# Attention units issued between the front products of the loop, and low halves of the first block kept off GpSimd

## Chip, core and metric

One Trainium2 chip, one NeuronCore. The metric is device time in microseconds (us), lower is better. The kernel is float32 throughout, with matrix products made from a high and a low float32r half of each operand.

## What is computed

Linear attention feeds two feed-forward layers. Per batch b and head h (8 x 8, sequence 576, head width 64):

```python
q_s = softmax(q, axis=-1)                  # over the 64 features
k_s = softmax(k, axis=2)                   # over the 576 positions
kv = einsum('bhsd,bhse->bhde', k_s, v)
x = einsum('bhsd,bhde->bhse', q_s, kv)     # heads side by side: 4608 x 512
x = (sigmoid(x @ w_gate) * (x @ w_val)) @ w_out        # 512 -> 1536 -> 512
h = x @ w_in                                           # 512 -> 2048
P = a0 + a1*h + a2*h**2 + a3*h**3;  Q = 1 + |b0|*|h| + |b1|*h**2
out = (P / (Q + 1e-6)) @ w_out2                        # 2048 -> 512
```

The weights arrive as float64; the kernel takes their bits apart on the chip.

## The kernel before

The 4608 tokens are cut into 9 blocks (j) of 512. A block of the first layer has 12 steps (f = 0 to 11, NF1 = 12). A step makes two front products, pg and pv, each summed over four chunks kk of the model width: 24 matmuls (`front_a`, 6 per chunk). ScalarE takes the sigmoid of pg, VectorE multiplies it with pv (the gate, L415), ScalarE rounds the result to its high half gh, and VectorE or GpSimd subtracts to get the low half gl (`vec_a`). The back product of the step before (12 matmuls, `back_a`) follows. pg and pv have two PSUM buffers in all, so the next step's front product can write pg only when the sigmoid has read it, and pv only when the gate has.

**The first block** and two blocks of attention are not written as a loop. Each piece of work is an op with predecessors, and a list scheduler at build time (`in_time`) puts them in order by a table of costs (`KINDS`). An op whose cost is a dict may go to VectorE or GpSimd: it takes the engine on which it would end first. That holds for k_sub, q_sub, q_div (softmax subtractions and divisions) and for the low halves w_l, g_l and next_l. In this block 36 weight pieces are unpacked: an absolute value on ScalarE, four bit operations on VectorE (L205, L208, L215, L218), a high half wh on ScalarE and a low half wl. The chosen engine shows at L472, which is the line of the helper that issues the op.

**The loop** runs steps i = 12 to 107. In step i the attention of a later block is worked on, four units u (pairs of heads) per block; `UNIT_STEPS` = 4, 6, 8, 10 sets the step d at which unit u is finished. All attention products share the two PSUM buffers of `ps_x`, in the order of issue. A unit has these parts: `load_k`, `load_q`, `load_v` (transfers on SP's queue), `att_km` (maximum of k, L287), `att_kt` (transpose ps_kt, then maximum mx L296 and a copy L298), `att_kb` (transpose back, then copy kma L306), `att_ks` (subtraction on GpSimd), `att_ke` (exponential of k, L327), `att_qm`, `att_qs`, `att_qe` (exponential of q, L319), `att_n` (four VectorE operations, L332 to L338), `att_kv` (20 matmuls, L353, L355, kvh on ScalarE, kvl on VectorE), `att_q` (four transposes ps_qt, high half qh, low half ql) and `att_d` (ps_xt and a copy into x_raw). The step issues them in this order:

```python
for kk in range(KC):
    front_a(f, kk, *ps)
vec = vec_a(j, f, *ps)
next(vec)                 # sigmoid
next(vec)                 # gate
run(sequence((), early_work.get(i, [])))                              # att_kt
run(prep(prep_at.get(i, [])), sequence(vec, work.get(i, [])))         # gh, gl, attention
if pend:
    back_a(*pend.pop(0))
run(sequence((), late_work.get(i, [])))                               # att_kb, att_ks
```

Beside it `prep` unpacks the 32 weight pieces of the second layer, spread over the loop; their low half hl is on GpSimd, and each is stored to memory by SP. The second layer follows the loop and is not touched.

Of the kernel before, what the change touches and what calls it, by code (L numbers as in the profile page):

```python
# [20 lines left out]
B, H, S, D = 8, 8, 576, 64  # L21
# [5 lines left out]
NF1, NF2 = F1 // P, F2 // P  # L27
# [11 lines left out]
PE, ACT, DVE, POOL, DMA = "PE", "ACT", "DVE", "POOL", "DMA"  # L39
# [8 lines left out]
    "x": (PE, 0.75), "x_h": (ACT, 0.6), "x_l": (DVE, 0.7),  # L48
    "xa": (PE, 0.65), "xa_out": (ACT, 0.25), "xb": (PE, 0.65), "xb_out": (ACT, 0.55),
    "w_abs": (ACT, 0.67), "w_clip": (DVE, 0.42), "w_cut": (DVE, 0.42), "w_low": (DVE, 0.7), "w_sign": (DVE, 0.7),  # L50
    "w_h": (ACT, 0.62), "w_l": ({DVE: 0.7, POOL: 1.29},),
    "front": (PE, 1.37), "sig": (ACT, 0.6, "sigmoid"), "gate": (DVE, 0.7), "g_h": (ACT, 0.63),
    "g_l": ({DVE: 0.7, POOL: 1.29},),
    "back": (PE, 2.73), "next_h": (ACT, 0.62), "next_l": ({DVE: 0.7, POOL: 1.29},),
}
LATENCY = {PE: 0.25, ACT: 0.2, DVE: 0.15, POOL: 0.15, DMA: 2.0}
TABLE_LOAD, TABLE_WEIGHT = 1.28, 2.0
# [61 lines left out]
def kernel(ctx: ExitStack, tc: tile.TileContext, q, k, v, w1, w2, ab_in, out):  # L119


    nc = tc.nc
# [9 lines left out]
    ps_x = ctx.enter_context(tc.tile_pool(name="ps_x", bufs=2, space=PSUM))  # L132
    dram = ctx.enter_context(tc.tile_pool(name="dram", bufs=1, space=DRAM))

    def f32(ap):
        return ap.bitcast(F32)
# [19 lines left out]
    w2_d = [dram.tile([P, 2, NB], F32, name=f"w2_{p}") for p in range(2 * NF2)]  # L156
    x3_d = [dram.tile([KC, P, NB], F32, name=f"x3_{j}") for j in range(NBLK)]

    def split_steps(h, lo, src, lo_eng):
        nc.scalar.activation(h, src, AF.Copy)  # L160
        yield
        lo_eng.tensor_tensor(out=lo, in0=src, in1=f32(h), op=ALU.subtract)  # L162
# [5 lines left out]
    def mm3(ps, wh, wl, xh, xl, first, last):  # L168
        nc.tensor.matmul(ps, wh, xh, start=first, stop=False)  # L169
        nc.tensor.matmul(ps, wl, xh, start=False, stop=False)  # L170
        nc.tensor.matmul(ps, wh, xl, start=False, stop=last)  # L171
# [13 lines left out]
    NW1, NW = 3 * NF1, 3 * NF1 + 2 * NF2  # L185
    raw, val, wt = {}, {}, {}
# [35 lines left out]
    def prep_split(p, eng=nc.gpsimd):  # L222
        if p < NW1:
            wt[p] = [wpool.tile([P, NB], F32R, tag="w", name=n) for n in ("wh", "wl")]
            yield from split_steps(*wt[p], val.pop(p), eng)
        else:
            hl = stage.tile([P, 2, NB], F32R, tag="raw", name="hl")
            yield from split_steps(hl[:, 0], hl[:, 1], val.pop(p), nc.gpsimd)
            yield
            nc.sync.dma_start(out=w2_d[p - NW1], in_=f32(hl))  # L230

    def fetch(p):
        wt[p] = [wpool.tile([P, NB], F32R, tag="w", name=n) for n in ("wh", "wl")]
        for n in range(2):
            nc.sync.dma_start(out=f32(wt[p][n]), in_=w2_d[p - NW1][:, n])

    def prep(stage_of):

        for p, n in stage_of:
            yield from (prep_load, prep_abs, prep_bits_a, prep_bits_b, prep_split)[n](p) or ()  # L240
            yield

    def mix(*jobs):
# [7 lines left out]
    def run(*jobs):  # L251

        jobs = list(jobs)
        while jobs:
            for x in list(jobs):
                if next(x, jobs) is jobs:
                    jobs.remove(x)

    def wa(f, i):
        return wt[at1[f, i]]  # L260
# [144 lines left out]
    def front_a(f, kk, pg, pv):  # L405
        for i, ps in enumerate((pg, pv)):
            wh, wl = wa(f, i)
            s = slice(kk * P, (kk + 1) * P)
            mm3(ps, wh[:, s], wl[:, s], x_h[:, kk, :], x_l[:, kk, :], kk == 0, kk == KC - 1)

    def vec_a(j, f, pg, pv):
        sg = tmp.tile([P, NB], F32, tag="t0", name="sg", bufs=1)
        nc.scalar.activation(sg, pg, AF.Sigmoid)  # L413
        yield
        nc.vector.tensor_tensor(out=sg, in0=pv, in1=sg, op=ALU.mult)  # L415
        yield
        gh = tmp.tile([P, NB], F32R, tag="gh", name="gh")
        gl = tmp.tile([P, NB], F32R, tag="gl", name="gl")
        g_t["a", j, f] = (gh, gl)
        late = nc.gpsimd if j == NBLK - 1 and f < NF1 - 1 else nc.vector  # L420
        yield from split_steps(gh, gl, sg, late if j else Chosen(("g_l", f)))

    def back_a(j, f):
        if f == 0:
            accs["a", j] = [ps_acc.tile([P, NB], F32, tag="acc", name="acc") for _ in range(KC)]
        gh, gl = g_t.pop(("a", j, f))
        wh, wl = wa(f, 2)
        for m, n in order(f == NF1 - 1):
            x, y = ((wh, gh), (wl, gh), (wh, gl))[n]
            nc.tensor.matmul(  # L430
                accs["a", j][m], x[:, m * P:(m + 1) * P], y, start=(f == 0 and n == 0),
                stop=(f == NF1 - 1 and n == 2))
        if f == NF1 - 1:
            for m, acc in enumerate(accs.pop(("a", j))):
                if m % 2:
                    nc.vector.tensor_copy(out=x_raw[:, m, :], in_=acc)  # L436
                else:
                    nc.scalar.activation(x_raw[:, m, :], acc, AF.Copy)
                nc.sync.dma_start(out=x3_d[j][m], in_=x_raw[:, m, :])
# [35 lines left out]
    for i in range(2 * NHP):  # L475
        j, u = divmod(i, NHP)
# [81 lines left out]
    for o in in_time(ops, chosen):  # L558
        ops[o][0]()

    work, early_work, late_work = {}, {}, {}

    def at(step, fn, *args):
        work.setdefault(max(step, NF1), []).append((fn, args))

    for j in range(2, NBLK):
        for u in range(NHP):
            d = NF1 * (j - 1) + UNIT_STEPS[u]
            if (j, u) != (2, 0):
                at(d - 5, load_k, j, u) if j < B else None  # L570
                at(d - 5, load_q, j, u)
            if j < B:
                at(d - 4, att_km, j, u)
                early_work.setdefault(max(d - 3, NF1 + 1), []).append((att_kt, (j, u, ps_x, "x")))
                late_work.setdefault(max(d - 3, NF1 + 1), []).append((att_kb, (j, u, ps_x, "x")))
                late_work[max(d - 3, NF1 + 1)].append((att_ks, (j, u, nc.gpsimd)))
                at(d - 2, att_ke, j, u)
                at(d - 3, load_v, j, u)
                at(d - 1, att_kv, j, u)
            at(d - 4, att_qm, j, u)  # L580
            at(d - 4, att_qs, j, u, nc.vector)
            at(d - 2, att_qe, j, u)
            at(d - 2, att_n, j, u, nc.vector)
            at(d - 1, att_q, j, u)
            at(d, att_d, j, u)

    def split_x():
        for kk in range(KC):
            split(x_h[:, kk, :], x_l[:, kk, :], x_raw[:, kk, :], nc.vector)

    def sequence(first, calls):
        yield from first
        for fn, args in calls:
            yield from fn(*args) or ()
            yield


    prep_at = {}
    for p in range(NW1, NW):
        at0 = NF1 + 2 + 5 * (p - NW1) // 2  # L600
        for n, step in enumerate((0, 1, 1, 2, 2)):
            prep_at.setdefault(at0 + step, []).append((p, n))

    NA = NBLK * NF1
# [1 line left out]
    for i in range(NF1, NA):  # L606
        j, f = divmod(i, NF1)
        ps = ps_f.tile([P, NB], F32, tag="f", name="pg"), ps_f.tile([P, NB], F32, tag="f", name="pv")
        for kk in range(KC):
            front_a(f, kk, *ps)  # L610
        vec = vec_a(j, f, *ps)
        next(vec)
        next(vec)
        if i == NF1:
            nc.scalar.activation(babs, ab[:, 4:6], AF.Abs)
        if i == NA - 1:
            nc.scalar.preload_act_table_set("natural_log_exp_and_others")
        if f == NF1 - 1:
            split_x()
        run(sequence((), early_work.get(i, [])))  # L620
        run(prep(prep_at.get(i, [])), sequence(vec, work.get(i, [])))
        if pend:
            back_a(*pend.pop(0))
        run(sequence((), late_work.get(i, [])))
        pend.append((j, f))
        if j == NBLK - 1 and f == 4:
            nc.sync.dma_start(out=x_raw, in_=x3_d[0].rearrange("m p c -> p m c"))
        if i == NA - NF1 - 2:
            att_ctx.close()
        if j == NBLK - 1:  # L630
            while len(wt) < NW and order1[len(wt) - NW1][0] < f - 1:
                fetch(len(wt))
# [84 lines left out]
    for i in range(NBS + LAG):  # L717
        while len(wt) < NW and i >= 0 and order1[len(wt) - NW1][0] < NF1 + i - 1:
            fetch(len(wt))
        if i < NBS:  # L720
            j, f = divmod(i, NF2)
# [57 lines left out]
```

## Time and profile before

| | us |
|---|---|
| median of 3 runs (range) | 1834.70 (1833.99 to 1836.22) |
| profiled execution, its own time | 1834.72 |
| its span, first to last instruction | 1832.9 |
| TensorE matmuls busy in the span | 1772.1 (97%) |
| VectorE busy | 1182.3 (65%) |
| ScalarE busy | 1005.6 (55%) |
| GpSimd busy | 363.3 (20%) |

PE is TensorE's matmuls, PEld its weight loads, DVE VectorE, ACT ScalarE, POOL GpSimd, SP the queue that issues transfers. A share of the whole span averages three stages that have different limits: the first block, the loop, and the second layer. Times of the trace count from the first instruction.

### The profile page before, as it was taken

To read this page: it belongs to the slowest core of one execution; us is meant where nothing else is said; L and a number is where in the kernel's file an instruction comes from. 1 tells how busy PE (TensorE), PEld (TensorE's weight loads), DVE (VectorE), ACT (ScalarE), POOL (GpSimd) and SP (SyncE) were. 2 spreads that over 40 slices of the span, in tenths; PEclk is the share of its full clock that TensorE was granted. 3 is DMA by queue.
4 is the path that set the end of the run, shared out by engine and by line. 5 is a ranking of instruction groups with operands and counts; after the bars stand their busy time and mean duration, and the time that the engine had idled before them with its cause. 6 is when DMAs were issued, how large, how long until landed. Compare 5 with 4: busy or idle time off the path is not lost.

```text
span 1832.9 us, 22295 instructions
## 1 busy us (share of the span) xinstructions
PE 1772.1 (97%) x8384; PEld 1452.7 (79%) x8384; DVE 1182.3 (65%) x1925; ACT 1005.6 (55%) x1652; POOL 363.3 (20%) x279
## 2 busy tenths in 40 slices
PE   5988999999999999999999999999999999999999
PEld 3766787787888878778888888888888888888887
DVE  9998545445455454454430288888888888887876
ACT  4556443444435354443331387777676777777765
POOL 3543010101011010110001122222222222222222
PEclk7999999999999999999999999999999999999999
DMA  6442323223132321312226401010000000000000
GB/s 206 146 150 89 115 68 107 69 64 114 62 123 75 110 79 54 123 61 84 78 77 212 160 24 43 5 47 12 35 23 24 24 24 24 23 24 24 1 24 23
DMA packets 53388, 129.54 MB, mean 71 GB/s; under 512 B 5664, under 2 KB 5664, under 8 KB 53280
## 3 DMA queue, kind: packets, MB, share of 16 engines
q1 hardware_dynamic: 53280, 128.12, 21.0%
q8 instruction: 66, 1.08, 0.2%
q14 instruction: 42, 0.34, 0.1%
HBM read 92.44 MB, written 35.65 MB: 70 GB/s over the span
## 4 chain that ended last, share of the span: by engine, by line
PE 56%; DVE 0%; ACT 0%; issue 0%
PE accb L698 21%; PE ph L171 7%; PE ph L170 7%; PE ph L169 7%; PE acc L430 4%; PE pg L169 1%; PE pv L169 1%; PE pg L171 1%; PE pv L171 1%; PE pg L170 1%; PE pv L170 1%; PE ps_qt L372 0%; PE ps_xt L170 0%; PE ps_xt L169 0%; PE ps_xt L171 0%; DVE km L287 0%
## 5 line engine op out<-in xcount | busy, mean ns | idle before, releaser
L415 DVE TENSOR_TENSOR sg<-pv,sg 128x512 f32<-128x512 f32 x108 | 74.4, 689 | 375.7 <-ACT sg L413 208.1
L162 POOL TENSOR_TENSOR glb<-gb,ghb 128x512 fp32r<-128x512 f32 x144 | 187.3, 1301 | 604.1 <-ACT ghb L160 585.4
L413 ACT ACTIVATE sg<-pg 128x512 f32<-128x512 f32 x108 | 64.5, 597 | 388.8 <-PE pg L171 387.0
L666 ACT ACTIVATE h<-ph 128x512 f32<-128x512 f32 x144 | 86.1, 598 | 196.9 <-PE ph L171 196.8
L169 PE MATMUL pg<-x_h,wh 128*128 128x512 f32 x432 | 172.1, 398 | 1.9 <-ACT sg L413 1.9
L169 PE MATMUL pv<-x_h,wh 128*128 128x512 f32 x432 | 169.3, 392 | 2.0 <-DVE sg L415 2.0
L170 PE MATMUL pv<-x_h,wl 128*128 128x512 f32 x432 | 168.9, 391 | 0.3 <-DVE wl L472 0.3
L171 PE MATMUL pv<-x_l,wh 128*128 128x512 f32 x432 | 168.9, 391 | 0.0
L170 PE MATMUL pg<-x_h,wl 128*128 128x512 f32 x432 | 168.8, 391 | 0.0
L171 PE MATMUL pg<-x_l,wh 128*128 128x512 f32 x432 | 168.7, 391 | 0.0
L698 PE MATMUL accb<-wh,ghb 128*128 128x512 f32 x576 | 158.3, 389 | 0.0
L698 PE MATMUL accb<-wl,ghb 128*128 128x512 f32 x576 | 158.3, 389 | 0.0
L698 PE MATMUL accb<-wh,glb 128*128 128x512 f32 x576 | 158.3, 389 | 0.0
L669 DVE SCALAR_TENSOR_TENSOR ah<-h,babs,ah 128x512 f32<-128x512 f32 x144 | 107.9, 750 | 54.5 <-ACT ah L667 54.5
L162 POOL TENSOR_TENSOR hl<-val,hl 128x512 fp32r<-128x512 f32 x32 | 41.3, 1290 | 475.1 <-ACT hl L160 224.3
L430 PE MATMUL acc<-gh,wl 128*128 128x512 f32 x432 | 122.4, 395 | 5.0 <-POOL wl L472 5.0
L430 PE MATMUL acc<-gh,wh 128*128 128x512 f32 x432 | 125.9, 402 | 0.4 <-DVE x_raw L436 0.3
L698 PEld LDWEIGHTS accb<-wl,ghb 128*128 128x128 f32 x576 | 108.1, 188 | 22.5
L698 PEld LDWEIGHTS accb<-wh,glb 128*128 128x128 f32 x576 | 108.1, 188 | 22.4
L698 PEld LDWEIGHTS accb<-wh,ghb 128*128 128x128 f32 x576 | 108.1, 188 | 22.4
L685 DVE SCALAR_TENSOR_TENSOR u<-ah,r 128x512 f32<-128x512 f32 x144 | 99.3, 690 | 39.5 <-ACT r L675 39.5
L169 PE MATMUL ph<-x_h,wh 128*128 128x512 f32 x320 | 124.5, 389 | 0.0
(129 smaller groups left out, 3974.5 us busy)
## 6 DMA issues: line engine op xcount, KB each, us to landing
raw<-in_w SPq DMA_DIRECT2D x68, 512.0 KB, 4.6
w<-hl SPq DMA_DIRECT2D x32, 512.0 KB, 2.9
v<-in_v SPq DMA_DIRECT2D x30, 325.0 KB, 3.3
k<-in_k SPq DMA_DIRECT2D x30, 320.0 KB, 4.1
q<-in_q SPq DMA_DIRECT2D x36, 256.0 KB, 4.2
x<-x_raw SPq DMA_DIRECT2D x36, 256.0 KB, 2.3
x_raw<-x SPq DMA_DIRECT2D x9, 1024.0 KB, 5.4
out<-ob SPq DMA_DIRECT2D x36, 256.0 KB, 2.3
```

The costliest lines, as they stand in the source:

```text
L162: lo_eng.tensor_tensor(out=lo, in0=src, in1=f32(h), op=ALU.subtract)
L169: nc.tensor.matmul(ps, wh, xh, start=first, stop=False)
L170: nc.tensor.matmul(ps, wl, xh, start=False, stop=False)
L171: nc.tensor.matmul(ps, wh, xl, start=False, stop=last)
L413: nc.scalar.activation(sg, pg, AF.Sigmoid)
L415: nc.vector.tensor_tensor(out=sg, in0=pv, in1=sg, op=ALU.mult)
L430: nc.tensor.matmul(accs["a", j][m], x[:, m * P:(m + 1) * P], y, start=(f == 0 and n == 0), stop=(f == NF1 - 1 and n == 2))
L666: nc.scalar.activation(h2, ph, AF.Square)
L669: nc.vector.scalar_tensor_tensor(out=ah, in0=h2, scalar=babs[:, 1:2], in1=ah, op0=ALU.mult, op1=ALU.add)
L685: nc.vector.scalar_tensor_tensor(out=u, in0=ah, scalar=q_one, in1=r, op0=ALU.add, op1=ALU.mult)
L698: nc.tensor.matmul(accs["b", j][t], x[:, t * P:(t + 1) * P], y, start=(f == 0 and n == 0), stop=(f == NF2 - 1 and n == 2))
```

## The change

In the loop, the early and the late list go away. Each attention part gets a step and a chunk kk, and is issued right after the six front matmuls of that chunk, ahead of the step's sigmoid and gate in every queue. The exponential and the subtraction of q move by a step, and the store of an unpacked weight piece becomes a stage of its own, a step later. In the cost table the low halves lose the choice of GpSimd.

```diff
-    "w_h": (ACT, 0.62), "w_l": ({DVE: 0.7, POOL: 1.29},),
+    "w_h": (ACT, 0.62), "w_l": (DVE, 0.7),
...
-    "g_l": ({DVE: 0.7, POOL: 1.29},),
-    "back": (PE, 2.73), "next_h": (ACT, 0.62), "next_l": ({DVE: 0.7, POOL: 1.29},),
+    "g_l": (DVE, 0.7),
+    "back": (PE, 2.73), "next_h": (ACT, 0.62), "next_l": (DVE, 0.7),
...
-            yield
-            nc.sync.dma_start(out=w2_d[p - NW1], in_=f32(hl))
+            val[p] = hl
+
+    def prep_store(p):
+        nc.sync.dma_start(out=w2_d[p - NW1], in_=f32(val.pop(p)))
...
-    def at(step, fn, *args):
-        work.setdefault(max(step, NF1), []).append((fn, args))
+    work = {}
+
+    def at(step, kk, fn, *args):
+        work.setdefault((step, kk) if step >= NF1 else (NF1, 0), []).append((fn, args))
...
-                at(d - 5, load_k, j, u) if j < B else None
-                at(d - 5, load_q, j, u)
+                at(d - 5, 2, load_k, j, u) if j < B else None
+                at(d - 5, 2, load_q, j, u)
             if j < B:
-                at(d - 4, att_km, j, u)
-                early_work.setdefault(max(d - 3, NF1 + 1), []).append((att_kt, (j, u, ps_x, "x")))
-                late_work.setdefault(max(d - 3, NF1 + 1), []).append((att_kb, (j, u, ps_x, "x")))
-                late_work[max(d - 3, NF1 + 1)].append((att_ks, (j, u, nc.gpsimd)))
-                at(d - 2, att_ke, j, u)
-                at(d - 3, load_v, j, u)
-                at(d - 1, att_kv, j, u)
-            at(d - 4, att_qm, j, u)
-            at(d - 4, att_qs, j, u, nc.vector)
-            at(d - 2, att_qe, j, u)
-            at(d - 2, att_n, j, u, nc.vector)
-            at(d - 1, att_q, j, u)
-            at(d, att_d, j, u)
+                at(d - 4, 1, att_km, j, u)
+                at(d - 3, 0, att_kt, j, u, ps_x, "x")
+                at(d - 3, 1, att_kb, j, u, ps_x, "x")
+                at(d - 3, 1, att_ks, j, u, nc.gpsimd)
+                at(d - 3, 2, load_v, j, u)
+                at(d - 2, 0, att_ke, j, u)
+                at(d - 1, 2, att_kv, j, u)
+            at(d - 3, 0, att_qm, j, u)
+            at(d - 3, 0, att_qs, j, u, nc.vector)
+            at(d - 3, 1, att_qe, j, u)
+            at(d - 2, 0, att_n, j, u, nc.vector)
+            at(d - 1, 2, att_q, j, u)
+            at(d, 0, att_d, j, u)
...
-        for n, step in enumerate((0, 1, 1, 2, 2)):
+        for n, step in enumerate((0, 1, 1, 2, 2, 3)):
...
             front_a(f, kk, *ps)
+            run(sequence((), work.get((i, kk), [])))
...
-        run(sequence((), early_work.get(i, [])))
-        run(prep(prep_at.get(i, [])), sequence(vec, work.get(i, [])))
+        run(vec, prep(prep_at.get(i, [])))
         if pend:
             back_a(*pend.pop(0))
-        run(sequence((), late_work.get(i, [])))
```

## Rows read from the trace of the kernel before

**Rows 1.** Busy time by stage: us, then each engine's busy us, granted clock, transfers.
```profile
0.00:30.00 30.00, 13.06 (x87) 8.40 (x87) 26.06 (x58) 14.50 (x28) 11.49 (x28) 0.85 0.70 244
30.00:165.00 135.00, 112.50 (x522) 87.26 (x523) 130.88 (x213) 74.78 (x125) 69.43 (x39) 0.92 0.45 146
165.00:965.00 800.00, 782.39 (x3967) 641.78 (x3967) 379.43 (x725) 333.56 (x558) 83.53 (x59) 1.00 0.26 85
...
1053.00:1832.90 779.90, 776.18 (x3425) 642.37 (x3423) 630.09 (x908) 561.15 (x907) 187.33 (x144) 1.00 0.07 24
```

**Rows 2.** Waits of TensorE, 165 to 1060 us: sum, times, longest.
```profile
PE ps_qt L372 <- DVE mx L296: 12.3, 18, 1.1
PE ps_kb L303 <- DVE kvl L364: 3.7, 7, 1.2
PE ps_qt L372 <- ACT x_raw L398: 0.5, 1, 0.5
```

**Rows 3.** Timeline of two loop steps, all engines: start, us, engine, line.
```profile
538.75 0.60 ACT L413 ACTIVATE sg<-pg 128x512 f32<-128x512 f32 x1 [2.18 <-PE pg L171]
...
539.43 0.80 PE L348 MATMUL ps_kv<-v,k 128*64 128x65 f32 x20
539.60 0.68 DVE L415 TENSOR_TENSOR sg<-pv,sg 128x512 f32<-128x512 f32 x1
...
540.63 0.63 PE L372 MATMUL ps_qt<-ident,q 128*128 128x128 f32 x4 [0.40 <-DVE mx L296]
...
542.59 0.15 DVE L353 TENSOR_SCALAR rs<-ps_kv 128x1 f32<-128x1 f32 x1
...
543.04 0.63 ACT L360 ACTIVATE kvh<-ps_kv,rs 64x64 fp32r<-64x64 f32 x2 [0.30 <-DVE rs L355]
543.69 0.60 ACT L377 ACTIVATE qh<-ps_qt 128x512 fp32r<-128x512 f32 x1
...
544.43 0.30 PE L303 MATMUL ps_kb<-ident,km 128*128 128x128 f32 x1 [0.43 <-DVE kvl L364]
...
552.25 1.28 ACT L327 ACT_TABLE_LOAD   x1
...
553.55 0.74 ACT L327 ACTIVATE k<-k 128x640 f32<-128x640 f32 x1
```

**Rows 4.** Chain of waits, two back products of steps without attention.
```profile
839.68 2.72 PE acc L430 x12
847.84 2.72 PE acc L430 x12
```

**Rows 5.** Transfers of k: KB each, median us from issue to landing.
```profile
k<-in_k SPq DMA_DIRECT2D x30, 320.0 KB, 4.1
```

**Rows 6.** Groups of instructions, 0 to 170 us: count, busy us, mean ns, idle before.
```profile
L215 DVE SCALAR_TENSOR_TENSOR early<-raw,early 128x512 uint32<-128x512 uint32 x34 | 31.8, 935 | 0.0
...
L472 POOL TENSOR_TENSOR wl<-early,wh 128x512 fp32r<-128x512 f32 x22 | 33.4, 1532 | 24.9 <-ACT wh L160 24.9
L472 POOL TENSOR_TENSOR gl<-sg,gh 128x512 fp32r<-128x512 f32 x10 | 25.2, 2525 | 22.6 <-ACT gh L160 22.6
```

**Rows 7.** Timeline of VectorE and GpSimd in the first block.
```profile
9.02 1.07 DVE L298 COPY km<-mx 128x128 f32<-128x128 f32 x1
...
70.20 0.68 DVE L218 SCALAR_TENSOR_TENSOR early<-raw,early 128x512 uint32<-128x512 uint32 x1
70.80 0.68 DVE L215 SCALAR_TENSOR_TENSOR early<-raw,early 128x512 uint32<-128x512 uint32 x1
...
71.63 1.34 POOL L472 TENSOR_TENSOR wl<-early,wh 128x512 fp32r<-128x512 f32 x1 [2.23 <-ACT wh L160]
71.74 1.77 DVE L218 SCALAR_TENSOR_TENSOR early<-raw,early 128x512 uint32<-128x512 uint32 x1
...
163.74 1.26 DVE L334 TENSOR_SCALAR qs<-qs 128x8 f32<-128x8 f32 x1
```

**Rows 8.** Waits of TensorE in the first block, 0 to 165 us.
```profile
PE acc L430 <- POOL wl L472: 5.0, 3, 2.0
```

More of the change, by code (lines that the diff above doesn't have):

```diff
@@ L239, in prep @@
         for p, n in stage_of:
-            yield from (prep_load, prep_abs, prep_bits_a, prep_bits_b, prep_split)[n](p) or ()
+            yield from (prep_load, prep_abs, prep_bits_a, prep_bits_b, prep_split, prep_store)[n](p) or ()
             yield
@@ L559 @@
         ops[o][0]()
-    work, early_work, late_work = {}, {}, {}
-    def at(step, fn, *args):
-        work.setdefault(max(step, NF1), []).append((fn, args))
+    work = {}
+    def at(step, kk, fn, *args):
+        work.setdefault((step, kk) if step >= NF1 else (NF1, 0), []).append((fn, args))
     for j in range(2, NBLK):
```

## The prediction, made before the changed kernel was run

> **What bounds the kernel now.** I read the busy times by stage first. In the second layer, from 1053 us, TensorE is busy 776.18 of 779.90 us and nothing of it is touched [rows 1]. In the loop, 165 to 965 us, it is busy 782.39 of 800: 17.6 us idle, with VectorE below half. From 30 to 165 us it is busy 112.50 of 135, 22.5 idle, and there VectorE is busy 130.88 of 135: VectorE sets the pace [rows 1]. Before 30 us TensorE is idle 16.9 us more. So the change can gain in two places: up to 17.6 us in the loop, and in the first block what it takes off VectorE.
>
> Next the waits of TensorE in the loop. Three make up 16.5 of the 17.6 us: the q transposes behind the maximum mx (12.3 us in 18 waits), the transpose back behind kvl (3.7 in 7), and the q transposes behind a copy (0.5) [rows 2]. They are waits for one of the two shared PSUM buffers. The timeline shows why: the products of k and v stand right behind the step's last front matmul, the q transposes 0.8 us behind them, and the maximum that must free the buffer stands behind the gate on VectorE (539.60 for 0.68 us); TensorE waits 0.40 us. The back transpose waits 0.43 us the same way [rows 3].
>
> **The loop, part by part.** *Removed: the buffer waits.* A step without attention takes 8.16 us (847.84 - 839.68), of which the back product is 2.72 [rows 4]; so a front matmul takes 5.44/24 = 0.227 us and a chunk of six 1.36. After the change att_kt, att_kb and att_kv with att_q stand 1.36 us apart or more, and att_d comes in the next step, behind a chunk, a back product and another chunk: 5.4 us. What releases each buffer is short: mx and its copy fit into the 1.36 us between att_kt and att_kb, provided VectorE is free; for the q transposes it is the copy kma, issued a chunk before. The gate of the step stands behind all this instead of ahead of it. I take all 16.5 us as removed.
>
> *Added: a longer way to the gate.* The step with att_kv now has the q exponential, kvh and qh ahead of the sigmoid on ScalarE, and the sigmoid's table load behind them. From the start of att_kv, by [rows 3]: products 0.80; about 0.05; rs to kvh 543.04 - 542.59 = 0.45; kvh to qh 0.65; qh 0.60; table load 1.28; sigmoid 0.60; gate 0.68; some 0.2 between engines: 5.3 us. Against it, TensorE has kv 0.80, the q transposes 0.4, chunk three 1.36 and the back product 2.72 before the next pg, and three pg matmuls (0.68) before the next pv [rows 3, 4]: pg at 5.3, where the sigmoid is done at 4.5; pv at 5.95, where the gate is done at 5.3. So some 0.65 us are left, and the added delay costs nothing. If that cover were gone, each us would count once in 28 steps (24 units with k and q, 4 with q alone).
>
> *Tables.* The exponentials of q and k stood together; now they are in two steps, each with a load of exp and one of sigmoid, 48 loads more. At 1.28 us each [rows 3] that is 61 us of ScalarE, which is busy 333.56 of 800 in the loop [rows 1]: hidden, outside of the chain above. After the load at 552.25 the exponential begins at 553.55, directly at its end [rows 3]. The Trainium skill, page "ScalarE: Activation LUTs", section "What ACT_TABLE_LOAD costs", puts a further drain of about 1.38 us to every switch, about 2.66 in all. This trace shows the load alone; the page's figure would take the rest of the cover and speak against the change (see the rivals).
>
> *Moved.* The q maximum and subtraction come a step later, behind att_kt on VectorE; who waits for them is the q exponential, behind it kvh and the sigmoid, in the chain above. The loads of v, k and q stand on SP's queue behind att_kv and ahead of the weight load; they still wait for the same buffers, and have most of a step (over 6 us) against 4.1 us to landing [rows 5] before the k maximum, so none should be late. The store of weight halves, a step later, blocks SP less. The k subtraction on GpSimd has a chunk and more before its exponential: no cost. One new collision is possible: hl on GpSimd (one in 2.5 steps) can hold up the copy between att_kt and att_kb, as in the rows below. By the times above hl ends just before; I take 0.5 us over the loop, and 10 meetings of up to 0.5 us as the bound. TensorE's instructions are the same, but a unit interrupts the front product in four places instead of three; 24 more interruptions cost between nothing and the 0.30 us of a transpose each, 7 us; I take nothing, since the transposes are only moved apart.
>
> Loop: -16.5 + 0.5 = -16 us; bounds -17.6 (all idle time) and -16.5 + 5 + 7 = -4.5.
>
> **The first block.** *Added to VectorE:* the low halves that are on GpSimd now, 22 wl and 10 gl [rows 6]; such instructions follow each other on VectorE by 0.60 us (70.20 to 70.80, [rows 7]): 32 x 0.60 = +19.2 us. *Given back:* the row at 71.74 shows the price of GpSimd's help. A bit operation takes 0.68 us at 70.20, and 1.77 us while wl is on GpSimd from 71.63 to 72.97: it waits nearly the whole GpSimd instruction, 1.09 us. The mean of this operation is 935 ns [rows 6]. I went through VectorE's timeline of the stage: 37 instructions take over 0.1 us more than the shortest of their kind, 35.3 us too long in sum (the first is the copy at 9.02, the last the addition at 163.74 [rows 7]); 26.6 us of it falls on low halves, the rest on k and q work. So -26.6 + 19.2 = -7.4 us. The Trainium skill, page "SBUF — State Buffer", section "Who interferes with whom", says that GpSimd shares a port pair with VectorE, and that whoever comes first holds it for a whole instruction; the row at 71.74 agrees.
>
> *The k and q work:* with the low halves gone GpSimd is free more often, and the scheduler gives it more subtractions and divisions. One of them frees 0.6 us of VectorE and can cost up to 1.09: about nothing in sum. The priorities rest on each op's lowest cost, which stays, so the plan is the same until the first low half that went to GpSimd; the idle time before 30 us stays. After that the order is a new one, which I did not work out. TensorE's waits for low halves from GpSimd (5.0 us in 3, [rows 8]; gl takes 2.53 us there [rows 6]) become waits for VectorE. Since VectorE is full and TensorE has 22.5 us idle, VectorE's gain shows in the end time; I take two thirds for what a new order loses: -5 us. Bounds: all 35.3 given back, -16; nothing given back, +19.2.
>
> **Sum.** -16 - 5 = -21 us. The profiled execution took 1834.72 us (span 1832.9 and 1.8 around it), the median is 1834.70: **1813.7 us**.
>
> **Rivals.**
> 1. *The first block gives nothing:* k and q work on GpSimd holds VectorE up instead, or TensorE's order is worse. For it: VectorE's gain is a difference of two larger numbers. 1834.7 - 16 = 1818.7.
> 2. *Small new waits in the loop:* the copy behind hl, or interruptions, 0.3 us in 28 steps: 1813.7 + 8.4 = 1822.
> 3. *The loop's waits only change their name* (the change doesn't do what it says): 1834.7 - 5 = 1829.7. Against it: the waits have one cause, which the distances of 1.36 us remove.
> 4. *The gate comes late (slower).* Place: the step with att_kv; price: 28 us for each us that the chain exceeds 5.95. It cancels the 21 us at 0.75 us over, a chain of 6.7 instead of 5.3. Two late switches of 1.3 us each, before the q exponential and before the sigmoid, would be such a case: the first has about 0.2 us of cover, the second 0.65, so some 1.8 us x 28 = 50 us, 1864. Against it: the exponential that follows its load directly. By the page's drain this would come out.
> 5. *VectorE pays in full (slower):* nothing is given back: 1834.7 - 16 + 19.2 = 1837.9. Against it: the 1.77 against 0.68.
>
> **How the numbers follow.** Forecast 0.68 (its own range 1807 to 1820), rivals 0.10, 0.10, 0.03, 0.05 and 0.04. The range 1806 to 1823 holds the forecast, the first two rivals and the nearer part of the bounds, and leaves out the other three and some overshoot. A measurement here tells 0.2% (3.7 us) from no change. Faster: forecast, rivals 1 to 3 and a small part of 4, 0.92; within 0.2%: parts of 4 and 5, 0.02; slower 0.06.
>
> **What would show it.** In the loop: TensorE busy over 798 of 800 us, the waits for mx and kvl gone, no wait of pg for the sigmoid or pv for the gate; the gate some 0.65 us before pv in steps with att_kv; 48 table loads more. In the first block: no wl or gl on GpSimd, L215 near 0.7 us in the mean, VectorE still nearly full, and the loop beginning some 5 us earlier. Wrong: waits behind the sigmoid every other step (rival 4), a loop that begins later (rival 5), or the new order leaving VectorE idle.

## The result, and the profile after

The changed kernel takes 1808.35 us (median of 4 runs, 1808.01 to 1810.34) against 1835.11 us; ratio 0.9856, 95% interval 0.9839 to 0.9874. It is 26.8 us faster; forecast were 21, to 1813.7 us, in a range of 1806 to 1823. The profiled execution took 1808.01 us, its span is 1806.2.

Busy time by stage, the same columns as [rows 1]:

```profile
0.00:30.00 30.00, 12.98 (x87) 8.45 (x87) 26.20 (x58) 14.50 (x28) 11.50 (x28) 0.85 0.70 244
30.00:165.00 135.00, 119.30 (x566) 93.22 (x567) 128.07 (x257) 81.76 (x136) 14.57 (x9) 0.91 0.45 146
165.00:965.00 800.00, 800.00 (x4040) 658.74 (x4039) 387.56 (x715) 399.88 (x603) 87.68 (x61) 1.00 0.27 92
```

In the loop TensorE is busy for all of the 800 us; no wait of TensorE is left between 165 us and the second layer, and those of [rows 2] are gone. From 30 to 165 us its idle time falls from 22.5 to 15.7 us; GpSimd is busy 14.57 us there instead of 69.43.

Where the 26.7 us of the spans come from is read off two starts, the first pg matmul of step 12 and the first ph matmul of the second layer. Timeline of TensorE, changed kernel:

```profile
167.76 0.50 PE L169 MATMUL pg<-x_h,wh 128*128 128x512 f32 x1
...
1016.22 0.39 PE L169 MATMUL ph<-x_h,wh 128*128 128x512 f32 x1
```

Before, these were at 174.40 and 1042.94. So the first block ends 6.6 us earlier, the loop takes 848.46 us instead of 868.54 (20.1 less), and the second layer is the same (790.0 us to the end of the span in both). Line numbers of the changed kernel stand two higher in this part of the program: its sigmoid is L415, its gate L417.

A loop step with att_kv, of the kind whose gate the prediction followed. Timeline, all engines, and below it the start and the sigmoid of a step whose unit is the fourth of its block:

```profile
517.20 0.27 PE L295 MATMUL ps_kt<-ident,km 128*128 128x128 f32 x1
...
517.50 0.29 DVE L298 TENSOR_REDUCE mx<-ps_kt 128x1 f32<-128x128 f32 x1 [1.22 <-PE ps_kt L295]
517.83 0.23 DVE L300 COPY km<-mx 128x128 f32<-128x128 f32 x1
...
518.69 0.27 PE L305 MATMUL ps_kb<-ident,km 128*128 128x128 f32 x1
...
520.27 0.80 PE L350 MATMUL ps_kv<-v,k 128*64 128x65 f32 x20
520.59 0.63 ACT L321 ACTIVATE q<-q 128x512 f32<-128x512 f32 x1
521.00 0.66 PE L374 MATMUL ps_qt<-ident,q 128*128 128x128 f32 x4
...
521.57 0.63 ACT L362 ACTIVATE kvh<-ps_kv,rs 64x64 fp32r<-64x64 f32 x2 [0.35 <-DVE rs L357]
522.23 0.60 ACT L379 ACTIVATE qh<-ps_qt 128x512 fp32r<-128x512 f32 x1
...
522.85 1.28 ACT L415 ACT_TABLE_LOAD   x1
...
524.14 0.60 ACT L415 ACTIVATE sg<-pg 128x512 f32<-128x512 f32 x1
...
524.77 0.69 DVE L417 TENSOR_TENSOR sg<-pv,sg 128x512 f32<-128x512 f32 x1 [1.22 <-ACT sg L415]
...
525.63 0.39 PE L169 MATMUL pg<-x_h,wh 128*128 128x512 f32 x1
...
576.40 0.80 PE L350 MATMUL ps_kv<-v,k 128*64 128x65 f32 x20
...
578.85 0.59 ACT L415 ACTIVATE sg<-pg 128x512 f32<-128x512 f32 x1
```

The copy of mx is done 0.6 us before the back transpose needs it. The gate ends at 525.46, 5.19 us after att_kv's start (5.3 forecast); the next pv starts at 526.31, 0.85 us later (0.65 forecast). The sigmoid begins 3.87 us after att_kv. With the fourth unit of a block it begins 2.45 us after it: no q exponential of a next unit falls into that step, and no table load stands ahead of the sigmoid. So the long chain exists in 21 of the 28 steps.

The first block, groups of instructions from 0 to 170 us:

```profile
L218 DVE SCALAR_TENSOR_TENSOR early<-raw,early 128x512 uint32<-128x512 uint32 x34 | 24.5, 727 | 0.0
L215 DVE SCALAR_TENSOR_TENSOR early<-raw,early 128x512 uint32<-128x512 uint32 x34 | 23.8, 706 | 0.0
L474 DVE TENSOR_TENSOR wl<-early,wh 128x512 fp32r<-128x512 f32 x34 | 22.2, 682 | 0.0
L208 DVE TENSOR_SCALAR early<-early 128x512 uint32<-128x512 uint32 x34 | 16.0, 482 | 0.0
L205 DVE TENSOR_SCALAR early<-early 128x512 f32<-128x512 f32 x34 | 14.1, 428 | 2.3 <-ACT early L199 2.3
...
L474 POOL TENSOR_TENSOR k<-k,kma 128x640 f32<-128x640 f32 x5 | 10.5, 2101 | 23.1 <-ACT kma L308 13.2 <-DVE early L218 7.5 <-DVE early L205 2.4
L474 POOL TENSOR_TENSOR q<-q,qm 128x512 f32<-128x512 f32 x7 | 8.9, 1266 | 99.3 <-DVE qm L313 76.3 <-PE ps_kt L295 7.9 <-PE acc L432 5.6
```

The bit operation L215 takes 706 ns instead of 935 [rows 6]. Before, L218, L205 and L208 took 898, 613 and 582 ns: the four together get back 685 ns a piece, 23 us over 34 pieces, and VectorE does all low halves. Counted as the prediction counted, in the first 165 us (instructions over 0.1 us longer than the shortest of their kind), the changed kernel has 9 left, 7.4 us too long in sum, all beside a k or q operation on GpSimd.

### The profile page after: what moved, and what is told of

It is laid out like the page before. It is cut to its first block, busy times and chain, and to the rows that moved or that the text cites. A ratio compares the mean times of both kernels' runs of the same rounds, so it can differ in the third digit from the quotient of the medians.

```text
span 1806.2 us, 22277 instructions
## 1 busy us (share of the span) xinstructions
PE 1769.7 (98%) x8384; PEld 1453.8 (80%) x8384; DVE 1185.7 (66%) x1956; ACT 1074.7 (59%) x1700; POOL 308.7 (17%) x248
## 4 chain that ended last, share of the span: by engine, by line
PE 93%; DVE 4%; DMA 1%; issue 1%; ACT 1%; SPq 0%; ACTq 0%
PE accb L703 22%; PE acc L432 15%; PE ph L171 7%; PE ph L169 7%; PE ph L170 7%; PE pg L169 5%; PE pg L170 5%; PE pv L170 5%; PE pv L169 5%; PE pg L171 5%; PE pv L171 5%; PE ps_kv L350 1%; PE ps_qt L374 1%; DMA raw<-in_w 1%; DVE early L215 1%
## 5 line engine op out<-in xcount | busy, mean ns | idle before, releaser
L417 DVE TENSOR_TENSOR sg<-pv,sg 128x512 f32<-128x512 f32 x108 | 74.6, 690 | 302.3 <-ACT sg L415 226.2
L169 PE MATMUL pg<-x_h,wh 128*128 128x512 f32 x432 | 177.2, 410 | 3.3 <-ACT sg L415 3.2
L415 ACT ACTIVATE sg<-pg 128x512 f32<-128x512 f32 x108 | 64.6, 598 | 173.8 <-PE pg L171 171.1
L170 PE MATMUL ph<-x_h,wl 128*128 128x512 f32 x320 | 124.5, 389 | 0.0
L171 PE MATMUL ph<-x_l,wh 128*128 128x512 f32 x320 | 124.5, 389 | 0.0
```

## Experiments

All ratios are to the kernel before, run on the same chip. Of each kernel the table has the start of the loop, the time from there to the second layer, and the measured time.

| kernel | loop starts | loop takes | median us | ratio (95%) |
|---|---|---|---|---|
| before | 174.40 | 868.54 | 1835.11 | 1 |
| changed | 167.76 | 848.46 | 1808.35 | 0.9856 (0.9839 to 0.9874) |
| loop_only | 172.85 | 848.48 | 1815.13 | 0.9897 (0.9883 to 0.9912) |
| costs_only | 169.41 | 868.21 | 1827.47 | 0.9965 (0.9950 to 0.9979) |
| half_wl_pool | 169.78 | 848.46 | 1812.86 | 0.9884 (0.9869 to 0.9899) |
| no_pool | 169.41 | 848.52 | 1811.01 | 0.9875 (0.9860 to 0.9890) |
| act_1 | 166.42 | 849.24 | 1810.53 | 0.9872 (0.9855 to 0.9888) |
| act_3 | 169.55 | 872.37 | 1833.22 | 0.9991 (0.9982 to 1.0000) |
| chunk_3 | 168.93 | 861.10 | 1821.76 | 0.9932 (0.9918 to 0.9947) |
| mx_first | 173.02 | 871.59 | 1837.92 | 1.0016 (1.0007 to 1.0026) |
| after_again | 169.92 | 848.44 | 1808.64 | 0.9853 (0.9839 to 0.9868) |
| all_wl_pool | 175.87 | 848.64 | 1815.33 | 0.9888 (0.9872 to 0.9905) |
| no_pool_again | 170.00 | 848.44 | 1812.45 | 0.9873 (0.9858 to 0.9888) |
| measured | 166.68 | 848.51 | 1805.89 | 0.9837 (0.9822 to 0.9852) |

The loop's length hardly varies between profiles of equal loops (848.44 to 848.64); the start of the loop does, by 3.5 us for the same first block (166.42 to 169.92).

**The two parts by themselves.** loop_only is the changed kernel with the old table:

```diff
-    "w_h": (ACT, 0.62), "w_l": (DVE, 0.7),
+    "w_h": (ACT, 0.62), "w_l": ({DVE: 0.7, POOL: 1.29},),
...
-    "g_l": (DVE, 0.7),
+    "g_l": ({DVE: 0.7, POOL: 1.29},),
```

(and next_l likewise). 

> The loop of the changed kernel with the cost table of before: low halves may go to GpSimd in the first block. If the two parts of the change add up as the trace divides them (6.6 us until the first step of the loop, 20.1 us in the loop), this takes 1834.7 - 20.1 = 1814.6 us, and its loop begins at 174.4 us as before. Rival: the new loop also helps the end of the first block (its last weight pieces run into the loop), then it is nearer to 1810.

costs_only is the kernel before with these three entries the other way round. 

> The cost table of the changed kernel with the loop of before. Two parts that add up: 1834.7 - 6.6 = 1828.1 us, the loop beginning near 167.8 us, and the waits for mx and kvl in the loop as before (16 us). Rival: the loop of before, with its lists after the gate, loses part of the 6.6 us again: 1830 or more.

Both times came out within 1 us of the forecast (1814.6 and 1828.1), the loops begin 1.6 us from it, and the two parts add up: 0.9897 x 0.9965 = 0.9862, against 0.9856 and 0.9853 for both. The loop gives 20 us whatever the first block does. The first block gives 6.4 us by the ratio of costs_only (3.9 to 9.2). By the profiles it gives 4.8: six with the new table and its plan (changed, after_again, costs_only, act_1, act_3, chunk_3) begin the loop at 168.7 in the mean, three with the old (before, loop_only, mx_first) at 173.4.

**The cover of the gate.** act_1 and act_3 repeat a copy on ScalarE ahead of the sigmoid, in the loop alone:

```diff
-        nc.scalar.activation(qh, tr, AF.Copy)
+        for _ in range(2 if j > 1 else 1):      # act_3: 4
+            nc.scalar.activation(qh, tr, AF.Copy)
```

> The changed kernel with the copy qh of the loop's att_q issued twice (ScalarE, 0.60 us more ahead of the sigmoid, 28 times). In the changed kernel the gate of such a step ends 5.19 us after the start of att_kv, the next pv begins at 6.04, and the sigmoid ends 4.47 against pg at 5.36. If the cover is real, 0.60 us fit into it: no change (within 2 us of 1808.4). Rival (the cover is already used up by waits that the profile hides): 28 x 0.6 = 17 us slower.

> The same with four copies in place of one: 1.80 us more ahead of the sigmoid. It then ends at 6.27 against pg at 5.36: 0.91 us late, and a listed wait of TensorE seems to cost some 0.16 us more than it shows, so 24 units x 1.07 = 26 us, 1834 us (the 4 units without k have a shorter chain). Rival (ScalarE's delay is hidden in another place, the gate is never late): no change.

act_1: the loop takes 849.24 us, 0.8 more; 28 x 0.6 us would be 17. Its median lies 2.2 us above the changed kernel's, with intervals that overlap. act_3: 23.9 us more in the loop (26 expected), the gain of the loop and more is gone. The waits of TensorE in act_3, 165 to 1060 us, and the timeline of one of them:

```profile
PE pg L169 <- ACT sg L416: 17.0, 21, 0.9
```

```profile
535.00 2.49 ACT L380 ACTIVATE qh<-ps_qt 128x512 fp32r<-128x512 f32 x4
...
537.50 1.07 PE L433 MATMUL acc<-gl,wh 128*128 128x512 f32 x4
537.50 1.28 ACT L416 ACT_TABLE_LOAD   x1
...
538.80 0.60 ACT L416 ACTIVATE sg<-pg 128x512 f32<-128x512 f32 x1
...
539.45 0.50 PE L169 MATMUL pg<-x_h,wh 128*128 128x512 f32 x1 [0.88 <-ACT sg L416]
539.79 0.39 PE L170 MATMUL pg<-x_h,wl 128*128 128x512 f32 x1
```

The sigmoid ends at 539.40, and pg follows. This row also shows how a listed wait is read. The last four back matmuls start at 537.50 and follow each other by 0.227 us [rows 4], so pg could have started at 538.41: it is 1.04 us late, and the profile lists 0.88. The modelled end of a matmul lies 0.39 us after its start, 0.16 us beyond the time at which the next could have begun. The matmul behind the wait is slow too: the next starts 0.34 us after it instead of 0.227.

The expected 26 us were 24 units at 1.07 us. That is near the measured 23.9, but the count was wrong, and the price left out what comes behind a wait. Step by step against the changed kernel, 18 steps are 1.05 us longer and three (units without k) 0.52; the steps of the fourth units are no longer than there; and each of the 21 steps behind a long chain is 0.16 us longer. Together these are 23.8 us.

**Where in the step.** chunk_3 issues att_kv and att_q after the last chunk, still ahead of the sigmoid:

```diff
-                at(d - 1, 2, att_kv, j, u)
+                at(d - 1, 3, att_kv, j, u)
...
-            at(d - 1, 2, att_q, j, u)
+            at(d - 1, 3, att_q, j, u)
```

> The changed kernel with att_kv and att_q issued one chunk later, after the last front matmuls and still ahead of the sigmoid and the gate. The cover shrinks by the chunk's 1.36 us: the sigmoid ends 4.47 us after att_kv's start, the next pg could begin at 1.2 + 2.72 = 3.95: 0.52 us late, 24 times, with 0.16 us unseen each: 16 us slower, 1824 us, and waits of pg for the sigmoid. Rival (what counts is only that attention stands ahead of the gate, not where): no change.

The time is 1821.76 us (1824 expected), and its loop takes 12.6 us more than the changed one's (16 expected). Waits of TensorE, 165 to 1060 us:

```profile
PE pg L169 <- ACT sg L415: 6.4, 18, 0.4
```

Here too it is 18 steps and not 24: they are 0.52 us longer each, 9.3 us, and the 21 steps behind a long chain 0.16 us each, 3.3 us. So with att_kv and att_q behind the last chunk the new loop gains 7.4 us; the chunk that covers the way to the gate is worth the other 12.6 of the 20.

**One wait of before, taken alone.** mx_first is the kernel before with att_kt ahead of the gate:

```diff
         next(vec)
-        next(vec)
+        run(sequence((), early_work.get(i, [])))
+        next(vec)
...
-        run(sequence((), early_work.get(i, [])))
         run(prep(prep_at.get(i, [])), sequence(vec, work.get(i, [])))
```

> The kernel before with one move: att_kt is issued between the sigmoid and the gate instead of behind the gate, so that the maximum mx that frees the PSUM buffer stands ahead of the gate on VectorE. If the waits come from the gate ahead of mx, the 12.3 us behind mx go, with some 0.16 us unseen for each of 18: 1834.7 - 15 = 1820 us. Rival (the distance between the products is what counts): under 5 us gained, the waits stay under mx or change their name.

My expectation failed: the kernel is no faster, its loop is 3.1 us longer. Waits of TensorE, 165 to 1060 us, and a timeline of one step:

```profile
PE ps_kb L303 <- DVE kvl L364: 13.4, 18, 1.7
PE ps_qt L372 <- DVE mx L296: 3.6, 8, 0.6
```

```profile
538.82 0.27 PE L293 MATMUL ps_kt<-ident,km 128*128 128x128 f32 x1
...
539.51 0.23 DVE L298 COPY km<-mx 128x128 f32<-128x128 f32 x1
539.65 0.68 DVE L415 TENSOR_TENSOR sg<-pv,sg 128x512 f32<-128x512 f32 x1
...
541.58 0.69 DVE L162 TENSOR_TENSOR gl<-sg,gh 128x512 fp32r<-128x512 f32 x1
...
542.18 0.15 DVE L353 TENSOR_SCALAR rs<-ps_kv 128x1 f32<-128x1 f32 x1
...
543.29 0.58 DVE L364 SCALAR_TENSOR_TENSOR kvl<-ps_kv,rs,kvh 64x64 fp32r<-64x64 f32 x2 [0.76 <-ACT kvh L360]
...
544.02 0.30 PE L303 MATMUL ps_kb<-ident,km 128*128 128x128 f32 x1 [0.84 <-DVE kvl L364]
544.07 0.48 PE L169 MATMUL pg<-x_h,wh 128*128 128x512 f32 x1
```

The same step in the kernel before, its first and its last row (the others are in [rows 3]):

```profile
539.23 0.27 PE L293 MATMUL ps_kt<-ident,km 128*128 128x128 f32 x1
...
544.48 0.49 PE L169 MATMUL pg<-x_h,wh 128*128 128x512 f32 x1
```

The q transposes no longer wait in this step, and the back transpose waits twice as long (0.84 us, 0.43 in [rows 3]). Its buffer is freed by kvl, which stands behind the gate, gl, rs and then kvh. From ps_kt to the next pg the step takes 5.25 us in both kernels: its length was set by kvl, and the listed wait for mx was only the first of two on the way there.

In the kernel before, that second wait is listed in 7 of the 18 steps. In the other 11 kvl was not late, and here the move itself made it late: mx and its copy now delay the gate (0.83 us after ps_kt, 0.37 before). Counted from ps_kt, in seven of these steps kvl starts 0.45 to 0.50 us later and the next pg 0.38 to 0.46 us; they make 3.0 of the 3.1 us. So 12.3 us behind mx became 3.6, and 3.7 us behind kvl became 13.4.

**The first block: lock or order.** The lock is what the row at 71.74 in [rows 7] shows: a VectorE instruction that waits while one of GpSimd runs. half_wl_pool and all_wl_pool keep the new plan and issue 18 or 36 of the weights' low halves on GpSimd:

```diff
-            (nc.vector if chosen[self.name] == DVE else nc.gpsimd).tensor_tensor(**kw)
+            gp = self.name[0] == "w_l" and self.name[1] % 2 == 0     # all_wl_pool: every piece
+            (nc.gpsimd if gp or chosen[self.name] != DVE else nc.vector).tensor_tensor(**kw)
```

> The changed kernel and its plan, but the low half of every second weight piece of the first block (18 of 36) is issued on GpSimd instead of VectorE, in the same place of the order. Theory of the lock: VectorE loses 18 x 0.60 = 10.8 us of work and waits 0.8 to 1.09 us for each, 14 to 20 us: 3 to 9 us slower than 1808.4. Rival (the plan's order made the gain, not the lock): VectorE is relieved and the time is the same or up to 10 us lower.

> The changed kernel and its plan, with the low half of all 36 weight pieces of the first block issued on GpSimd. With 18 of them the time was a few us over the changed kernel, near the limit of what the intervals tell. By the lock: VectorE loses 36 x 0.60 = 21.6 us and waits 0.8 to 1.09 us for each, 29 to 39 us: 7 to 18 us slower than its neighbour. Rival (the order of the plan, not the lock, makes the first block's gain): the same time or less.

all_wl_pool is 6.7 us slower than its neighbour after_again, just under the 7 to 18 expected, and its loop begins 6 us later. The plan is the same, so the rival in its strong form is out: the order alone does not carry the gain. Whether a plan made for low halves on GpSimd would do better is not tested. Half of them cost 4.5 us against the changed kernel's first runs, with intervals that overlap. But the size has another split than expected. Busy time of all_wl_pool, groups from 0 to 165 us, and waits from 30 to 165 us:

```profile
30.00:165.00 135.00, 112.59 (x532) 86.58 (x533) 119.36 (x209) 78.36 (x128) 65.22 (x43) 0.95 0.46 146
```

```profile
L218 DVE SCALAR_TENSOR_TENSOR early<-raw,early 128x512 uint32<-128x512 uint32 x34 | 26.0, 770 | 0.0
L215 DVE SCALAR_TENSOR_TENSOR early<-raw,early 128x512 uint32<-128x512 uint32 x34 | 25.8, 765 | 0.0
L205 DVE TENSOR_SCALAR early<-early 128x512 f32<-128x512 f32 x34 | 20.3, 609 | 5.7 <-ACT early L199 5.7
L208 DVE TENSOR_SCALAR early<-early 128x512 uint32<-128x512 uint32 x34 | 19.0, 570 | 0.1
```

```profile
DVE sg L417 <- ACT sg L415: 3.4, 4, 1.3
...
ACT early L199 <- POOL wl L475: 3.7, 5, 1.7
```

The bit operations are slowed again: against 684, 684, 421 and 420 ns in no_pool_again, where GpSimd has none of this work, 505 ns a piece and 17 us in all. That is less than the 21.6 us VectorE is relieved of. VectorE is busy 119.36 us (126.27 in after_again) and idle 15.6 instead of 8.7. Part of the new idle time is lateness: in this kernel ScalarE waits 3.7 us for buffers that a low half on GpSimd has yet to free, and VectorE's gate waits 3.4 us for the sigmoid; after_again lists neither. What makes the sigmoid late I did not trace. So a low half on GpSimd is paid for in two ways, as VectorE's lock and as lateness, and here the lock alone would not have made the kernel slower.

**No GpSimd at all.** no_pool takes GpSimd out of the entries for k_sub, q_sub and q_div:

```diff
-    "k_cp": (ACT, 0.33), "k_sub": ({DVE: 0.83, POOL: 1.55},), "k_exp": (ACT, 0.74, "exp"),
+    "k_cp": (ACT, 0.33), "k_sub": (DVE, 0.83), "k_exp": (ACT, 0.74, "exp"),
```

(q_sub and q_div likewise). 

> The changed kernel with no work of the first block on GpSimd at all: the 15 subtractions and divisions of k and q that it still has there go to VectorE too. By the lock one of them costs VectorE 0.6 to 0.8 us and gives back up to 1.09: 15 x 0.65 = 10 us against at most 16: between 6 us faster and 5 slower, most likely within 3 us. Rival (an offload is an offload, with waits of its own that cost VectorE nothing): 10 us slower.

> The changed kernel with no subtraction or division on GpSimd in the first block, against its neighbour, since the first run (1811.0) and the changed kernel's (1808.4) were not taken together. If what GpSimd still does is about even for VectorE, within 2 us of the neighbour; if it is a real help, 3 us or more slower.

1811.0, and 1812.5 beside a changed kernel of 1808.6: 3.8 us slower in direct comparison (medians; the intervals overlap). The two profiled executions begin the loop at the same time (170.00 and 169.92 us). What GpSimd keeps in the changed kernel is worth some 3 us, if anything.

These kernels also show the lock most plainly. Counted as above, VectorE has 38 instructions that are too long in the kernel before (36.1 us in sum, 27.3 of it beside low halves; the prediction had 37, 35.3 and 26.6), 30 in all_wl_pool (24.1), 9 in the changed kernel (7.4), and none in no_pool and no_pool_again.

**A better table.** measured sets VectorE's and GpSimd's costs to the start-to-start times of the trace:

```diff
-    "w_abs": (ACT, 0.67), "w_clip": (DVE, 0.42), "w_cut": (DVE, 0.42), "w_low": (DVE, 0.7), "w_sign": (DVE, 0.7),
+    "w_abs": (ACT, 0.67), "w_clip": (DVE, 0.335), "w_cut": (DVE, 0.335), "w_low": (DVE, 0.6), "w_sign": (DVE, 0.6),
```

(and so on for 19 VectorE costs and the three shared ones). 

> The changed kernel with the table's VectorE and GpSimd costs set to what the trace shows from start to start (0.60 for 0.70, 0.335 for 0.42, GpSimd's k subtraction 2.1 for 1.55 and so on). If the first block is bound by VectorE's sum of work, a better order can only take away what TensorE and VectorE wait there: within 3 us of the neighbour, either way. Rival (the plan's order leaves much): 5 us or more faster.

1805.9 us (1804.1 to 1807.1) beside 1808.6 (1807.7 to 1810.1): 2.7 us lower, the lowest median of all, with no overlap of the runs but with ratio intervals that overlap. The expectation holds; that it beats the changed kernel is likely and not shown.

## Why the prediction was right, and which term was off

**The loop's waits: right in kind, 4 us too small.** All three waits of [rows 2] are gone and nothing came in their place. The mis-sized step is "I take all 16.5 us as removed", with its bound of 17.6 us as "all idle time": the loop got 20.0 us shorter (loop_only, and the changed kernel 20.1). Counted by the starts of TensorE's matmuls instead of by listed waits, the sum closes. In the loop before, the q transposes began 13.6 us late (12.3 listed), the back transposes 4.8 (3.7 listed), six transposes ps_kt 1.1 (0.2 listed, for km), and one back product behind a copy to x_raw 1.0 (0.3 listed). That is 20.4 us. In the step of [rows 3] the q transposes start 1.20 us after att_kv (539.43 to 540.63), in the changed kernel 0.73 (520.27 to 521.00): 0.47 late, where 0.40 is listed. So about 2.4 us were hidden in the two waits that count, 2.1 lay in smaller waits that the prediction left out, and its third wait (0.5) lies ahead of the loop's first step. The 0.16 us that I carried from one wait to all holds behind 512-column matmuls; behind att_kv it is 0.07.

**The cause as I told it was incomplete.** The prediction put the waits down to mx standing behind the gate. mx_first shows that this place alone is worth nothing: kvl, behind the gate and gl, sets the length of some of these steps already and of others as soon as mx goes ahead. With all of VectorE's attention work ahead of the gate and the products a chunk or more apart, every wait is gone. No run separates the order on VectorE from the distance between the products. chunk_3 shows the worth of the cover alone. Rival 3, that the waits only change their name, is what a part of this change would have done.

**The gate's longer way: right for the step it followed, too many such steps.** 5.19 us against 5.3 forecast, 0.85 us of cover against 0.65. act_1 shows that 0.6 us of it can be used up for 0.8 us in the loop; act_3 that 1.8 us can't. Rival 4 counted 28 steps for each us beyond the cover; it is 21, because the fourth unit of a block has no q exponential and no table load in its step. In act_3 a late step costs its delay and some 0.16 us more in the step behind. The 48 table loads are there and cost nothing: the next activation begins at the load's end, as at 522.85 and 524.14 above. The further drain of about 1.38 us that the Trainium skill (page "ScalarE: Activation LUTs", section "What ACT_TABLE_LOAD costs") adds to a switch is not seen; here the measurement decides.

**hl on GpSimd against the copy; four interruptions instead of three:** both taken at next to nothing, and right. The waits that went make 20.4 us and the loop is 20.1 shorter, so all that was added to it, these two included, costs about 0.3 us in sum.

**The first block: right in size, partly by luck.** -5 us were forecast; 4.8 by the profiles, 6.4 by costs_only. VectorE got back 23 us on the bit operations alone and, counted as the prediction counted, 27.3 us on low halves (26.6 forecast); it took over 33 low halves at 0.60 us, 20 us (19.2 forecast); GpSimd took two more k and q operations (15 instead of 13). VectorE's idle time from 30 to 165 us rose from 4.1 to 6.9 us, part of what the forecast allowed for a new order. The two thirds that turned -7.4 into -5 were a guess, and the start of the loop varies by 3.5 us between profiles, so the agreement to 1 us is luck. Rival 1 (nothing gained) and rival 5 (VectorE pays in full) are out. all_wl_pool shows that the lock is not the only price of work on GpSimd. How the 5 to 6 us divide between the lock, lateness and the new order stays open.

## What to carry to other kernels

Where several products share few buffers, the wait that the profile names first may not be the one that sets the length: ask what the next user of the same buffers waits for, and what the moved piece will push back; then move all releasing work, not one piece. Sum the late starts of matmuls rather than the listed waits. Attention-like side work is best placed between parts of the main product, ahead of the step's own post-processing, as long as the longer way to that post-processing fits into what TensorE still has to do; that margin can be worked out from a timeline and tested with one repeated instruction. Count in which steps the long way exists. Give GpSimd work that VectorE's instructions do not meet in the meantime, and count on both prices when they do.

## What the runs showed of the hardware

VectorE can hold GpSimd off for long. In the kernel before, a low half that takes 1.28 us on GpSimd at 159.99 took over four times as long at 96.87, while VectorE's instructions followed each other without a gap up to 101.14. Timeline of GpSimd and VectorE, kernel before:

```profile
96.87 5.43 POOL L472 TENSOR_TENSOR gl<-sg,gh 128x512 fp32r<-128x512 f32 x1 [3.96 <-ACT gh L160]
...
100.73 0.41 DVE L208 TENSOR_SCALAR early<-early 128x512 uint32<-128x512 uint32 x1
101.36 1.22 DVE L205 TENSOR_SCALAR early<-early 128x512 f32<-128x512 f32 x1 [0.22 <-ACT early L199]
...
159.99 1.28 POOL L472 TENSOR_TENSOR wl<-early,wh 128x512 fp32r<-128x512 f32 x1 [1.35 <-ACT wh L160]
```

The GpSimd instruction ends at 102.30, 1.16 us after VectorE's first pause since 96.87 began, and VectorE's next instruction takes 1.22 us (0.41 for the same line at 99.79). That fits GpSimd doing its work from that pause on, and VectorE then waiting for it; the other two long low halves (4.13 us at 59.44, 5.10 at 76.74) have no such pause inside, so it is not shown as a rule.

I had expected GpSimd's price on VectorE (1.09 us, [rows 7]) and not that the same conflict can cost GpSimd 4 us the other way. It is one source of the low halves' lateness in the first block (gl took 2.53 us in the mean, [rows 6]); how much of the lateness it explains I did not measure.
